# Quarter products in the free row tile of the score fills, and a narrower hold on VectorE's score tiles

## The chip, the cores and the metric

The kernel runs on one core of one Trainium2 chip. The metric is the device time of one execution in microseconds (us); the median of three runs before the change is 734.45 us (734.43 to 736.88). The core has five engines with instruction queues of their own: TensorE (PE in the profile) multiplies matrices into the accumulator memory PSUM, whose eight banks hold 128 x 512 float32 values each; ScalarE (ACT) applies functions such as exp; VectorE (DVE) does elementwise work and copies; GpSimd (POOL) does integer adds here; SyncE (SP) issues most of the DMAs. They meet at semaphores.

## The reference

Two layers are computed on separate inputs and joined along the last axis, each for 2048 positions and width 640. The first is a state-space layer: a complex diagonal recurrence over time between two dense products, plus a skip term. The second is attention with 32 query heads of width 20 that share one key and one value head.

```python
    Lam_bar = jnp.exp(dt * Lam)
    B_bar = ((Lam_bar - 1.0) / Lam)[:, None] * Bmat
    Bu = jnp.einsum("bld,pd->blp", x + 0j, B_bar)
    for t in range(L):
        h = Lam_bar[None, :] * h + Bu[:, t, :]
        hs.append(h)
    y = 2.0 * jnp.einsum("blp,dp->bld", hseq, Cmat).real + x * Dskip[None, None, :]
...
    q = (x @ wq) split into 32 heads of 20;  k = x @ wk;  v = x @ wv
    scores = jnp.einsum("bhqd,bkd->bhqk", q, k) * (Dh ** -0.5)
    p = _softmax(scores, axis=-1)
    o = jnp.einsum("bhqk,bkd->bhqd", p, v)
    b = (heads of o joined) @ wo
...
    return jnp.concatenate([a, b], axis=-1)
```

## The kernel before, in words

**Score tiles.** Attention is cut into 2048 score tiles of 128 keys x 512 queries: four blocks of 512 queries, eight groups of four heads, sixteen key chunks, four heads. A head needs only 20 (plus one) of the 128 input rows of TensorE, so the four heads of a group lie in four bands of 32 rows of the tiles KT and QT, and a score matmul uses one *row tile*: 32 rows by 128 columns of the array (32*128 in the profile). `fill` issues the score matmuls of two or three tiles, in different row tiles, into one of two PSUM slots (SC, three banks each).

**Two ways to exp.** Either ScalarE applies exp to a slot (L1213, PR<-SC: 1024 or 1536 columns for two or three tiles). Or VectorE turns the score into the bits of a power of two in int16 (`fill_d`, BIG<-SC); three further shifted copies follow, on GpSimd two tiles at a time (L1507) or on VectorE, and the weighted sum of the four approximates exp. The names with `_d` and the third tile of a slot called `own` stand for this. A tile done by ScalarE needs one value product, one done by VectorE needs four. Value products use *column tiles*, 128 rows by 32 columns (128*32), four heads side by side (`pv`, MB<-PR,VP and MB<-BIG,VS), and add up in one bank, `pvbank`.

**Everything else on TensorE** runs in column tiles too: `mm` splits a product with 128 output rows into four matmuls of 32. These are the products of generator tasks: `q_task` (queries, 5 steps of 128 input rows each), `unit_task` (input of the recurrence for one of four time blocks and one of five state chunks: 10 steps for each of real and imaginary part), `cb_task` (a product of C and B, 10 steps), `y_task` (output of the state-space layer, up to 16 steps, where the fifth of each block, k = 4, handles the last 128 columns), `o_task` (output projection, 5 steps), and some small ones. Each holds a PSUM bank (MB) until VectorE has copied it out. Two single banks are left beside the slots: `pvbank`, and one for all tasks (`misc`).

**The order of all instructions is written out before the run.** `Schedule` simulates the engines with estimated durations, picks by priority what each engine does next, and the `Emitter` writes every engine's stream and the semaphore waits. Score fills have priority 0, tasks 0.95, value products 2.0 (0.9 when they are urgent). An operation has a mode, S for row tiles and C for column tiles, and changing the mode has a price in the plan. Tasks come up by the number of score tiles issued (`tile_n`), the state-space work between tiles 260 and 1780; `planned` tries several random shifts of these times (`PLANS`, 4) and keeps the plan that ends first by its own clock.

**How many tiles VectorE gets.** `want_own` and `want_d` allow one when the count stays under `SHARE` (0.28) of the tiles, when buffers are free, when fewer than two first steps wait, and when `behind()` is false. `behind()` (L1273) is true while the closing step W of the next state-space unit hasn't started and `tile_n` is more than 120 tiles (`LAG`) past that unit's due time. VectorE steps of a unit have low priority until `hurry` marks them `late`, 40 tiles after the due time (scaling of C: from tile 150).

Of the kernel before, what the change touches and what calls it, by code (L numbers as in the profile page):

```python
# [23 lines left out]
class Op:  # L24
# [3 lines left out]
                 "seq", "land", "dma_key", "idx", "tail", "mode", "load", "late", "port", "after", "due", "table", "psum")  # L28

    def __init__(self, eng, fns, dur, deps=(), prio=5, reads=(), writes=(), prev=None, gate=None, hook=None,  # L30
# [7 lines left out]
        self.port, self.after, self.due, self.table = port, [], None, None  # L38
# [213 lines left out]
class Emitter:  # L252
# [11 lines left out]
    def plan(self):  # L264
# [8 lines left out]
        for op in self.order:  # L273
# [12 lines left out]
            for o in op.after:  # L286
                dep(o)
            for k in op.writes:
                for k2 in self.shares.pop(k, ()):
                    dep(last_w.get(k2))  # L290
                    for r in readers.get(k2, ()):
                        dep(r)
# [55 lines left out]
        for e in ("pe", "act", "dve", "pool"):  # L348
            v = 0
            for op in self.streams[e]:  # L350
                if op.dma_key is None and id(op) in needed:
                    v += 1
                    self.value[id(op)] = v
# [4 lines left out]
    def emit(self, block):  # L358
        def run(e, be):
            for op in self.streams[e]:  # L360
# [6 lines left out]
                for fn in op.fns:  # L367
                    ins = fn(be)
                    if op.dma_key is not None:
# [14 lines left out]
class Bank:  # L384
# [7 lines left out]
    def cols(self, lo, hi):  # L392
        return self.tensor[:, self.off + lo:self.off + hi]

# [21 lines left out]
class Build:  # L416
# [7 lines left out]
    SHARE = 0.28  # L424
# [66 lines left out]
    PLANS = 4  # L491
# [149 lines left out]

    @staticmethod
# [12 lines left out]
    def program(self):  # L655
# [7 lines left out]
        self.tasks = []  # L663
        self.evac_op, self.norm_op, self.part_op = {}, {}, {}
# [362 lines left out]
    def q_task(self, qb, blk, bank):  # L1027

        p = self
        prev = None  # L1030
        for c in range(NC):
            at = 640 * c + 128 * blk
            prev = self.pe([self.mm(bank.ap, p.wqf[:, at:at + 128], p.xbT[:, c, 512 * qb:512 * qb + 512], c == 0, c == NC - 1)],
                           self.mmt(512), deps=[self.wqa_op, self.wq_op, self.xb_op[qb, c]] + bank.last, prev=prev,
                           prio=self.task_prio(), reads=[f"xbT{qb}_{c}", "wqa", "wqb"], writes=[bank.key])
# [143 lines left out]
    def fill(self, op, i):  # L1179
# [27 lines left out]
        for m in extra:  # L1207
            self.fill_d(op, m)
        op.reads = sorted(set(op.reads))
        op.dur = self.mmt(512, len(op.fns))  # L1210
        op.load = 128.0 * len(op.fns)
# [61 lines left out]
    def behind(self):  # L1273

        while self.next_unit < NQB * NC:
            w = self.w_op.get(divmod(self.next_unit, NC))
            if w is None or w.start is None:
                return self.tile_n > self.unit_due[divmod(self.next_unit, NC)] + self.LAG
# [405 lines left out]
    def o_task(self, qb, k, bank, early=False):  # L1684
# [28 lines left out]
        for i in range(begin, upto):  # L1713
            if last:
                yield lambda: all(n in self.norm_op for n in steps[i][0])
            prev = part(i, prev, i == begin)
        if early:
# [273 lines left out]
    def cb_task(self, cd, h, pc, ld, made, bank):  # L1991
        p = self
        prev = None
        n = 0
        for c in range(NC):
            for ri in range(2):
                prev = self.pe([self.mm(bank.cols(0, 320), pc[:, c, ri, :], p.CT[:, ri, c, 320 * h:320 * h + 320], n == 0, n == 2 * NC - 1)],
                               self.mmt(320), deps=[ld] + self.c_scaled + bank.last, prev=prev, prio=self.task_prio(),
                               reads=[f"pc{cd % 2}", f"CT{ri}_{c}"], writes=[bank.key])
                n += 1  # L2000
# [8 lines left out]
    def unit_task(self, tb, c, bank):  # L2009
        p = self  # L2010
        u = (tb * NC + c) % 2
        prev = None
        lo = 256 * (tb % 2)
        for ri in range(2):
            terms = [(eo, cd) for eo in range(2) for cd in range(NC)]
            for n, (eo, cd) in enumerate(terms):
                t, k, op = (p.BT, "BT", self.bt_op) if eo else (p.BA, "BA", self.ba_op)
                prev = self.pe([self.mm(bank.cols(256 * ri, 256 * ri + 256), t[:, ri, cd, 128 * c:128 * c + 128], p.xaT[:, cd, eo, lo:lo + 256],
                                        n == 0, n == 2 * NC - 1)], self.mmt(256),
                               deps=self.xa_op[tb] + [op[ri][cd]] + bank.last, prev=prev,  # L2020
                               prio=self.task_prio(), reads=[f"{k}{ri}_{cd}", f"xaT{tb % 2}_{cd}_{eo}"], writes=[bank.key])
# [68 lines left out]
    def y_task(self, tb, k, bank):  # L2090
# [3 lines left out]
        prev = None  # L2094
        rows_of = range(4) if k == 4 else [k]
        lo, hi = (512, 640) if k == 4 else (0, 512)
        W = p.W[tb % 2]
        for r in rows_of:
            i, eo = divmod(r, 2)
            o0 = 128 * r if k == 4 else 0  # L2100
            to = bank.cols(o0, o0 + hi - lo)
            x0 = 256 * (tb % 2) + 128 * i
            at = 1 + 128 * i + eo
            n = 0
            for c in range(NC):
                for ri in range(2):
                    m, mk = (p.CT, f"CT{ri}_{c}") if eo else (p.CA, f"CA{c}")
                    prev = self.pe([self.mm(to, W[:, c, ri, at:at + 128], m[:, ri, c, lo:hi], n == 0, False)],
                                   self.mmt(hi - lo), deps=deps, prev=prev,
                                   prio=self.task_prio(), reads=[f"W{c}_{tb % 2}", mk], writes=[bank.key])  # L2110
                    n += 1
            if not eo:
                for cd in range(NC):
                    prev = self.pe([self.mm(to, p.xaT[:, cd, 0, x0:x0 + 128], self.cb_of(cd, lo, hi), False, False)],
                                   self.mmt(hi - lo), deps=deps, prev=prev, prio=self.task_prio(),
                                   reads=[f"xaT{tb % 2}_{cd}_0", f"CB{cd}"], writes=[bank.key])
# [182 lines left out]
```

## Time and profile before

| | |
|---|---|
| median of 3 runs | 734.45 us |
| profiled execution: time, and its span | 734.64 us, 732.8 us |
| busy: PE, ACT, DVE, POOL | 708.3, 712.4, 602.0, 408.8 us |
| exponentials on ScalarE, L1213 | 679 |
| score matmuls, 32*128 | 2048 |
| value products, 128*32: MB<-PR,VP and MB<-BIG,VS | 1526 and 2088 |
| first steps on VectorE, BIG<-SC, 128x512 int16 | 485 |
| granted TensorE clock | 0.993 |

The page gives busy time and the chain that ended last; groups are listed as line, engine, operation, output<-input by tile name (buffer numbers left out), shape and count, then busy time, mean duration of one, idle time before them and what ended it. A table by stretch gives the window and its length, the busy time and count, the granted clock, and two DMA figures. In order of time, a row is: start, length, engine, line, operation, tiles, the tile of the array (rows*columns), shape, how many in a row. Line numbers are often those of helpers: L637 is the plain matmul, L633 the one split into four column tiles, L647, L651 and L652 are VectorE's elementwise helpers. A matmul's shown length of about 0.39 us includes the pipeline; the distance between starts tells what it occupies.

### The profile page before, as it was taken

What the parts mean: (1) busy time and instruction counts of PE and PEld (TensorE: products, weight loads), DVE (VectorE), ACT (ScalarE), POOL (GpSimd) and SP (SyncE); (2) the same over time, 40 slices, a digit from 0 to 9 for tenths busy, and PEclk for the clock granted to TensorE, in tenths of its full rate; (3) what the DMA queues carried; (4) which work ended last, traced back from release to release, by engine and by line L of the source; (5) the groups of instructions that cost most, each with busy time, mean ns of one, the idle gap of its engine ahead of it and who ended that gap; (6) DMA issues with size and microseconds to landing.
All of it is one profiled execution on the core that took longest, in us unless ns stands there. A gap on an engine that the chain in (4) does not pass through costs nothing.

```text
span 732.8 us, 26675 instructions
## 1 busy us (share of the span) xinstructions
PE 708.3 (97%) x11268; PEld 253.0 (35%) x11271; DVE 602.0 (82%) x1178; ACT 712.4 (97%) x703; POOL 408.8 (56%) x686
## 2 busy tenths in 40 slices
PE   8999999998999999999999999999999999999997
PEld 4322223233443432333333333233333333342233
DVE  7767999897677697778988998988889998876873
ACT  6899999999999999999999999999999999999995
POOL 3366564530046377586663746566645665687860
PEclk9799999999999999999999999999999999999999
DMA  9403543366121010100110010101100001100001
GB/s 204 68 27 107 133 110 99 76 138 97 31 60 26 13 30 24 38 23 18 40 41 23 16 26 26 42 21 34 34 20 10 19 8 40 37 24 18 19 21 38
DMA packets 78090, 34.44 MB, mean 47 GB/s; under 512 B 58852, under 2 KB 77972, under 8 KB 77972
## 3 DMA queue, kind: packets, MB, share of 16 engines
q1 hardware_dynamic: 76352, 32.34, 18.6%
q8 instruction: 90, 1.47, 0.8%
q10 hardware_dynamic: 1620, 0.39, 0.3%
q14 instruction: 28, 0.23, 0.1%
HBM read 11.53 MB, written 9.75 MB: 29 GB/s over the span
## 4 chain that ended last, share of the span: by engine, by line
ACT 52%; PE 45%; DVE 2%; DMA 1%; issue 1%; ACTq 0%
ACT PR L1213 51%; PE MB L637 16%; PE SC L637 15%; PE MB L633 12%; PE SC L633 1%; DMA BIG<-in_B_wq_dram 1%; DVE prod L647 0%; DVE BIG L652 0%; DVE mab L887 0%; DVE pvsb L647 0%; PE SC L929 0%; ACTq L618 0%; DVE g L2041 0%; DVE QT L652 0%; DVE pvsb L1574 0%
## 5 line engine op out<-in xcount | busy, mean ns | idle before, releaser
L1213 ACT ACTIVATE PR<-SC 128x1024 bf16<-128x1024 f32 (+1 forms) x679 | 697.5, 1239 | 5.1 <-PE SC L637 3.6
L1507 POOL INT64_ADD BIG<-BIG x659 | 397.9, 619 | 292.5 <-DVE BIG L652 171.8
L652 DVE TENSOR_SCALAR BIG<-SC 128x512 int16<-128x512 f32 x485 | 325.8, 686 | 70.1 <-PE SC L637 64.3
L637 PE MATMUL SC<-QT,KT 32*128 32x512 bf16 x2011 | 267.1, 386 | 14.6 <-ACT PR L1213 10.1
L637 PE MATMUL MB<-BIG,VS 128*32 128x512 bf16 x2088 | 244.0, 384 | 0.0
L637 PE MATMUL MB<-PR,VP 128*32 128x512 bf16 x1526 | 211.6, 386 | 0.5 <-DVE pvsb L1574 0.3
L637 PEld LDWEIGHTS SC<-QT,KT 32*128 32x128 bf16 x2011 | 68.0, 91 | 254.4 <-ACT PR L1213 178.1
L637 PEld LDWEIGHTS MB<-BIG,VS 128*32 128x32 bf16 x2088 | 59.1, 95 | 64.8 <-issue 47.3
L637 PEld LDWEIGHTS MB<-PR,VP 128*32 128x32 bf16 x1526 | 51.6, 95 | 54.8 <-issue 41.5
L652 DVE TENSOR_SCALAR BIG<-BIG 128x1024 int16<-128x1024 int16 (+1 forms) x136 | 48.8, 405 | 7.6 <-PE MB L637 5.7
L633 PE MATMUL MB<-CT,W 128*32 128x320 bf16 (+2 forms) x1040 | 51.4, 301 | 0.8 <-DVE prod L647 0.5
L633 PE MATMUL MB<-xaT,BT 128*32 128x256 bf16 x800 | 35.4, 275 | 0.0
L647 DVE TENSOR_TENSOR prod<-MB,tab 128x1024 bf16<-128x1024 f32 x20 | 24.3, 1217 | 13.0 <-PE MB L633 12.9
L633 PE MATMUL MB<-xaT,BA 128*32 128x256 bf16 x800 | 32.7, 274 | 0.0
L633 PE MATMUL MB<-CA,W 128*32 128x512 bf16 (+1 forms) x640 | 32.0, 302 | 0.7 <-issue 0.4
L652 DVE TENSOR_SCALAR BIG<-MB 128x512 int16<-128x512 f32 x37 | 25.2, 682 | 3.7 <-PE MB L637 2.4
L633 PE MATMUL MB<-WO,OP 128*32 128x128 bf16 (+1 forms) x576 | 27.8, 297 | 0.2 <-DVE pvsb L647 0.2
L633 PEld LDWEIGHTS MB<-CT,W 128*32 128x32 bf16 x1040 | 20.9, 96 | 18.2 <-issue 10.2
L633 PE MATMUL MB<-BIG 128*32 128x512 bf16 x340 | 26.7, 397 | 0.0
L1755 DVE CAST stg<-MB 128x512 bf16<-128x512 f32 x35 | 23.9, 683 | 1.7 <-PE MB L633 1.3
L1574 DVE CAST pvsb<-MB 128x512 bf16<-128x512 f32 x31 | 21.2, 684 | 3.8 <-PE MB L637 3.7
L2041 DVE TENSOR_TENSOR_SCAN g<-sc,hst,prod 128x256 bf16<-128x256 f32 x30 | 22.3, 754 | 0.1
(162 smaller groups left out, 388.2 us busy)
## 6 DMA issues: line engine op xcount, KB each, us to landing
out_dram<-stg SPq DMA_DIRECT2D x31, 128.0 KB, 1.8
qd<-BIG SPq DMA_DIRECT2D x20, 128.0 KB, 1.9
QT<-qd SPq DMA_DIRECT2D x28, 80.0 KB
OP<-pvsb SPq DMA_DIRECT2D x105, 20.0 KB
rdP<-recs SPq DMA_DIRECT2D x105, 20.0 KB
W<-in_A_B_re_dram SPq DMA_DIRECT2D x10, 160.0 KB, 2.6
W<-in_A_B_im_dram SPq DMA_DIRECT2D x10, 160.0 KB, 2.6
lbd<-W SPq DMA_DIRECT2D x10, 160.0 KB, 2.4
```

Source lines behind the costliest of these rows:

```text
L633: r = e.matmul(out[32 * j:32 * j + 32], lhsT=lhsT[:, 32 * j:32 * j + 32], rhs=rhs, start=start, stop=stop, tile_position=(0, 32 * j), skip ...
L637: return lambda e: e.matmul(out, lhsT=lhsT, rhs=rhs, start=start, stop=stop, **kw)
L647: return lambda e: e.tensor_tensor(out, a, b, op)
L652: return lambda e: e.tensor_scalar(out, a, s1, s2, op0=op0, op1=op1)
L1213: ex = self.act(lambda e: e.activation(dst, t[:, 0:512 * n], ACT.Exp, scale=1.0 / UNIT), 0.8333 * 512 * n + 64, table="exp", deps=[op], re ...
L1507: op.fns.append(lambda e: e.int64_add(words(dst), words(src), add))
L1574: ev = self.dve(lambda e: e.tensor_copy(p.pvsb[:, slot, :], bank.ap), 645, deps=[op], reads=[bank.key], writes=[f"pvsb{slot}", f"pvsb{slot ...
L1755: ev = self.dve(lambda e: e.tensor_copy(st, bank.ap), 645, deps=[prev], reads=[bank.key], writes=[key], prio=self.EV, gate=(lambda: last.e ...
L2041: o = self.dve(lambda e, ri=ri, init=init: e.tensor_tensor_scan(p.g[:, u, ri, :], rdec, p.prod[:, 1, 0, ri, :], init, ALU.mult, ALU.add), ...
```

## The change

A task of `q_task`, `o_task` (all but the last query block), `cb_task`, `unit_task` and `y_task` hands its steps to a new generator `ride`. It issues them from the front in column tiles, as before, in pieces of up to 256 columns. In addition `fill` calls `board` once its own tiles are chosen: if a row tile is still free, a step from the *back* of the list may be opened and split into four quarters of 32 input rows. One quarter, in the free row tile, joins the fill: its first matmul ahead of the scores, the others after them. A step is opened only when the product has begun, more than `KEEP_C` = 5 steps are left and none is open (`OPEN` = 1). When the steps run out, the task waits for the fills to take the quarters that are left; after 2500 ns of plan time (`PATIENCE`) one goes alone (`alone`). Consecutive quarters of a product write the same bank from different row tiles, so each waits on TensorE's own semaphore for the former (`fence`). Where a quarter has several matmuls, the operation increments its semaphore twice, at the last score and at the last matmul (`twice`), and waits of others count both. `behind()` gets a second condition. `SHARE` becomes 0.29 and `PLANS` 8. In `unit_task` and the narrow `y_task` the order of the terms changes, since a step now holds both parts or all four row blocks.

```diff
+            if op.fence is not None:
+                need[e] = op.fence
...
-                    v += 1
+                    v += 1 if op.twice is None else 2
...
-                for fn in op.fns:
+                for x, fn in enumerate(op.fns):
                     ins = fn(be)
+                    if x == op.twice and id(op) in self.needed:
+                        ins.then_inc(self.sems[e], 1)
...
-    SHARE = 0.28
+    SHARE = 0.29
...
-    PLANS = 4
+    PLANS = 8
...
+    GRAIN, KEEP_C = 256, 5
+    def ride(self, bank, steps):
+        p = self
+        r = Ride(bank, [[list(m), list(deps), list(keys)] for m, deps, keys in steps])
+        self.rides.append(r)
+        def hook(op):
+            mms, _, keys = r.steps[0]
+            n = 0
+            while mms and (not n or n + mms[0][2].shape[-1] <= p.GRAIN):
+                out, lhsT, rhs = mms.pop(0)
+                n += rhs.shape[-1]
+                op.fns.append(p.product(r, out, lhsT, rhs, range(4), r.last is None))
+                r.last = op
...
+        while r.open:
+            t0 = self.s.t
+            self.s.at(t0 + self.PATIENCE)
+            op = self.pe([], self.mmt(512), prio=1.5, mode="S", load=128.0, writes=[bank.key], hook=lambda op: self.alone(r, op),
+                         gate=lambda: bool(r.open) and self.s.t >= t0 + self.PATIENCE - 1.0)
...
+    def piece(self, r, out, lhsT, rhs, row):
...
+        at = slice(32 * row, 32 * row + 32)
+        return lambda e: e.matmul(out, lhsT=lhsT[at], rhs=rhs[at], start=False, stop=r.end is tag,
+                                  tile_position=(32 * row, 0), skip_group_check=True)
+    def board(self, op, used):
...
+            if best is None and rows and len(r.steps) > self.KEEP_C and len(r.open) < self.OPEN:
+                step = r.steps[-1]
+                if all(d.end is not None and s.seen(d, "pe") <= s.t for d in step[1]):
+                    best = [r.steps.pop(), set(range(4))], rows[0]
+                    r.open.append(best[0])
...
+            fns = [self.piece(r, *m, x) for m in step[0]]
+            if len(fns) > 1:
+                op.twice = len(op.fns)
+            op.fns[:] = fns[:1] + op.fns + fns[1:]
...
+            self.rode(r, op, x)
...
+    def rode(self, r, op, row):
+        if r.rode is not None:
+            op.fence = r.rode
+        r.rode = r.last = op
...
+        n_mm = len(op.fns)
+        self.board(op, used)
         op.reads = sorted(set(op.reads))
-        op.dur = self.mmt(512, len(op.fns))
-        op.load = 128.0 * len(op.fns)
+        op.dur = self.mmt(512, n_mm + (len(op.fns) > n_mm))
+        op.load = 128.0 * n_mm
...
-                return self.tile_n > self.unit_due[divmod(self.next_unit, NC)] + self.LAG
+                return self.tile_n > self.unit_due[divmod(self.next_unit, NC)] + self.LAG \
+                    and any(o.late and self.s.ready(o) is not None for o in self.s.pending["dve"])
...
+        prev = yield from self.ride(bank, [
+            ([(bank.ap, p.wqf[:, 640 * c + 128 * blk:640 * c + 128 * blk + 128], p.xbT[:, c, 512 * qb:512 * qb + 512])],
+             [self.wqa_op, self.wq_op, self.xb_op[qb, c]], [f"xbT{qb}_{c}", "wqa", "wqb"]) for c in range(NC)])
...
+        prev = yield from self.ride(bank, [
+            ([(bank.cols(0, 320), pc[:, c, ri, :], p.CT[:, ri, c, 320 * h:320 * h + 320])],
+             [ld] + self.c_scaled, [f"pc{cd % 2}", f"CT{ri}_{c}"]) for c in range(NC) for ri in range(2)])
...
+                steps.append(([(bank.cols(256 * ri, 256 * ri + 256), t[:, ri, cd, 128 * c:128 * c + 128],
+                                p.xaT[:, cd, eo, lo:lo + 256]) for ri in range(2)],
...
+        prev = yield from self.ride(bank, steps)
```

## The prediction

> **What bounds the kernel now.** I read the page first: the busy line, the chain that ended last, and the costliest groups.
>
> ```profile
> PE 708.3 (97%) x11268; PEld 253.0 (35%) x11271; DVE 602.0 (82%) x1178; ACT 712.4 (97%) x703; POOL 408.8 (56%) x686
> ...
> ACT 52%; PE 45%; DVE 2%; DMA 1%; issue 1%; ACTq 0%
> ```
>
> Two engines are full, and the chain passes from one to the other. ScalarE has hardly a hole: the exponentials (L1213) show 5.1 us idle in 697.5 busy. How they are split decides the time, so next the groups kept apart by shape:
>
> ```profile
> L1213 ACT ACTIVATE PR<-SC 128x1024 bf16<-128x1024 f32 x509 | 480.5, 1119 | 4.9 <-PE SC L637 3.6 <-PE MB L637 0.3
> ...
> L652 DVE TENSOR_SCALAR BIG<-SC 128x512 int16<-128x512 f32 x485 | 325.8, 686 | 70.1 <-PE SC L637 64.3 <-PE MB L637 0.9 <-POOL BIG L1507 0.2
> ...
> L1213 ACT ACTIVATE PR<-SC 128x1536 bf16<-128x1536 f32 x169 | 236.9, 1606 | 0.2 <-PE MB L637 0.2
> ```
>
> A fill brings three score tiles. Either ScalarE takes all three (1536 columns), or two, and VectorE the third (1024). ScalarE took 1526 of the 2048 tiles (2 x 509 + 3 x 169 + 1), so VectorE took 522. Then the stages. GpSimd's adds (L1507), which follow every VectorE tile, by stretch, and the exponentials from 153.8 to 202 and from 460 to 700:
>
> ```profile
> 20.00:153.00 133.00, 72.58 (x120) 0.96 0.36 90
> 153.00:203.00 50.00, 0.12 (x1) 1.00 0.43 88
> 203.00:480.00 277.00, 168.81 (x280) 1.00 0.12 29
> 480.00:720.00 240.00, 156.42 (x259) 1.00 0.09 23
> ...
> L1213 ACT ACTIVATE PR<-SC 128x1536 bf16<-128x1536 f32 x37 | 49.8, 1712 | 0.0
> ...
> L1213 ACT ACTIVATE PR<-SC 128x1024 bf16<-128x1024 f32 x201 | 188.4, 1115 | 1.0 <-PE SC L637 0.6
> L1213 ACT ACTIVATE PR<-SC 128x1536 bf16<-128x1536 f32 x41 | 58.3, 1554 | 0.2 <-PE MB L637 0.2
> ```
>
> For 50 us VectorE gets no score tile at all: `behind()` (L1273) holds them back. There a fill takes 49.8/37 = 1.346 us. From 460 to 700, where 201 of 242 fills (83%) have a VectorE tile, a fill of 1024 takes (240 - 41 x 1.346)/201 = 0.92. **So each tile moved to VectorE takes 0.42 us from ScalarE.** Last, TensorE in order of time:
>
> ```profile
> 360.30 0.39 PE L637 MATMUL SC<-QT,KT 32*128 32x512 bf16 x3
> 360.62 0.39 PE L637 MATMUL MB<-PR,VP 128*32 128x512 bf16 x1
> ...
> 361.17 0.39 PE L637 MATMUL SC<-QT,KT 32*128 32x512 bf16 x3
> 361.18 0.38 PE L637 MATMUL MB<-QT,KT 32*128 32x512 bf16 x1
> 361.49 0.39 PE L637 MATMUL MB<-PR,VP 128*32 128x512 bf16 x2
> ...
> 404.41 0.39 PE L637 MATMUL SC<-QT,KT 32*128 32x512 bf16 x3
> 404.64 0.38 PE L637 MATMUL MB<-QT,KT 32*128 32x512 bf16 x1
> 404.94 0.39 PE L637 MATMUL MB<-PR,VP 128*32 128x512 bf16 x2
> ...
> 654.49 0.83 PE L637 MATMUL MB<-BIG,VS 128*32 128x512 bf16 x12
> 655.25 0.39 PE L637 MATMUL SC<-QT,KT 32*128 32x512 bf16 x3
> ```
>
> Three score matmuls of 32 rows start together; 0.32 us later the column-tiled work starts (360.62). A group of four column matmuls takes (0.83 - 0.39)/2 = 0.22 (0.217 over longer runs), and from the last group's start to the next fill is 0.32, that is 0.10 for the change of tiling. A fourth row tile (361.17) leaves the distance at 0.32 (361.49): the free row costs under 0.01 us. From 203 to 720 TensorE shows 511 us busy of 517, so there it binds as well; from 153 to 203 it ran 164 dummy matmuls to stay warm.
>
> **The change, part by part.** *Hold.* From the starts of the 20 closing steps of the state-space units (W<-prod) and the number of score matmuls begun by then, `behind()` was true for 111 us in all. The new condition also wants a late VectorE step whose forerunners have started. From 153.8 to 178.0 VectorE works through exactly such a chain (scaling of C), and between a unit's rotation (prod<-MB) and its W another one stands ready. What is left open is where VectorE waits for TensorE: 178.0 to 181.4, 186.2 to 189.7, 194.2 to 197.6, 241 to 248.4, 386.4 to 389.5 and 527 to 532, about 25 us. That is 25/1.346 = 18.6 fills, of which 83% get a VectorE tile: 15 x 0.42 = **-6.5**. Ends: 0 if something late is always ready; all 111 us (82 fills, 68 tiles), but the new share 0.29 x 2032 = 589 allows 67: -28. I take the value of the gaps, since the timeline shows them.
>
> *Rides.* A quarter of a step leaves the column-tiled stage and goes in a fill's free row. 628 of 679 fills have just three row tiles. A step can be opened only after the product's first step and while more than five are left (KEEP_C = 5), one at a time (OPEN = 1). Query and output products have five steps, so by the code **they never ride**. For the others I took each product's matmuls, counted the fills between its steps, and opened a step by that rule: 20 units give 80 rides, the 10 CB products 28, the 16 wide y products 104, the four narrow ones 24: 236. A ride saves a quarter of 0.217, so 0.054 (CB, 320 columns: (0.85 - 0.30)/4/4 = 0.034): 208 x 0.054 + 28 x 0.034 = 12.2 us, less 236 x 0.004 for the fourth row, 11.2 us of TensorE; 28 of them lie before 203, where it isn't full: 10 us count. ScalarE is full too, so it must be exchanged: a 1024 fill with its VectorE tile costs TensorE 0.32 + 0.10 + 1.5 groups = 0.745, a 1536 fill 0.32 + 0.10 + 0.75 groups = 0.583, so one exchange needs 0.163 more TensorE in a round that is 0.42 shorter: 0.58. 10/0.58 = 17 exchanges x 0.42 = **-7**. What hides the new VectorE work: 32 tiles x 0.686 = 22 us more on an engine with 131 us idle, and 48 adds x 0.62 = 30 on GpSimd with 292 idle. Without that cover nothing is won here.
>
> A ride of a unit is two matmuls of 256 in one row tile, of the diagonal and the narrow products up to four of 128, and the exponential waits for the last one (two increments). Below: full-array matmuls of 128 columns, new weights each, ran 16 in 1.07 us, (1.07 - 0.22)/15 = 0.057, so four take 0.23, as long as a score. Above: the one kind of fill here with a late fourth matmul (404.41, fourth at 404.64, next group 404.94) took 0.53 instead of 0.32, so 0.21 a ride. I take the lower, a row with the same column counts, and keep 0.21 for the range.
>
> A rule of the Trainium skill speaks against this part ("TensorEngine Tiling (Array Packing)", Instruction Overhead): every matmul carries an overhead of some 60 cycles, so no tiling factor should come out of a dimension that is already small. At the 2.4 GHz of the table in "TensorE: Matmul & The Clock Gate" that is 25 ns; for some 580 pieces of 128 to 512 columns I estimate 14.5 us, so that the rides would cost TensorE 3 us instead of saving 11, and the sum would end near 731. The measured 0.057 for 128 columns is only 4 ns above 128 cycles at that clock, so I go by the row.
>
> *Waits.* Each ride waits on TensorE for the ride before (fence); behind it stand the fill, and for that ScalarE. The former fill's matmuls end 0.39 after their start and fills are 0.87 or more apart, so 0; above, 0.1 each if the release is late, 24. Quarters left when the steps run out wait 2.5 us (2.7 fills) for a matching free row, then run alone for 0.22; the row left out is the one with most tiles left and comes first next time, so I take 5, **+1**; a quarter of all would be +13. Meanwhile the one spare bank is held, and the next product with its evacuation and output DMA on SP waits; the code adds or moves no other DMA.
>
> *Share 0.28 to 0.29* binds only from about 60 to 110 us (D share 0.25 to 0.27 of the tiles): 0.01 x 300 = 3 tiles, **-1**. *Eight plans for four*: the planner takes the best by its own clock; 0 to -2, I take 0. Finer steps (256 columns at a time) issue the same matmuls: 0.
>
> **Sum**: the profiled execution took 734.64 (span 732.8, 1.8 around it), 0.2 over the median 734.45. 734.6 - 6.5 - 7 - 1 + 1 = **721**.
>
> **Rivals.** (1) *VectorE takes everything*: with the hold gone and TensorE relieved, the share is reached: 67 x 0.42 = 28, so 706 to 711. For it: outside the hold 83% of fills already have a VectorE tile. Against: VectorE would get to (602 + 46)/706, 92%, and TensorE needs 67 x 0.58 = 39 us for it.
> (2) *Pieces in one row tile do not overlap* (slower): the fill grows by up to 0.21, 236 rides, and the next exponential is late. From 0.10 a ride on it loses: 236 x (0.10 - 0.05) = 12, more than the hold's 7.5 and the 0.5%; 0.11 gives 741, 0.21 765. For it: the fill at 404.41. Against: the 0.057 row.
> (3) *The units slip* (slower): the hold also kept most units at 100 to 150 tiles behind their due times, and no more. The last y product now ends at 708.6, the last exponential at 722.6: 14 us of room. A slip of over 80 us, a full block of five y products after the last score (5 x 16 x 0.217 + 3 = 20), gives 741.
> (4) *Nothing is exchanged*: the freed TensorE time becomes dummy work and something late is always ready, so the hold stays: 730 to 734.
>
> **How the numbers follow.** The forecast 0.55 (its own range 714 to 728), rival 1 0.15, rival 2 0.10, rival 3 0.07, rival 4 0.13. About 0.5% (3.7 us) is what a measurement can tell from no change. Faster by more: 0.55 + 0.15 + 0.05 of rival 4 = 0.75; within: 0.08; slower: 0.17. The range must reach from rival 1 to the near end of rivals 2 and 3: 706 to 740, which leaves out most of rival 2 and some of rival 3, some 0.13.
>
> **What would show it.** Exponentials of 1024 columns rise from 509 to some 545, those of 1536 fall to about 145; GpSimd's adds no longer vanish from 178 to 203 but still do from 154 to 178. Some 240 quarters appear as 32*128 matmuls of W, xaT, CA, CT in fills, none of wq or WO, and fills with them still take 0.32 to the next group. Wrong if such fills take 0.4 or more, if y products stand after the last exponential, or if the 1024 count stays below 515.

## The result, and the profile after

The changed kernel takes **728.31 us** (median of 4, 727.54 to 729.73) against 734.55 before (median of 4): a ratio of **0.990, 95% interval 0.987 to 0.993**, 6.2 us less by the medians, 7.2 by the ratio. The forecast was 721: the direction is right, the gain about half of what was forecast (13.5).

**The clock of an execution.** The executions of one kernel don't all run at the same granted TensorE clock, and their times follow it. The 25 executions of the kernel before that were measured with four of the experiments took 738.1 to 738.8 us at 0.986, 735.7 to 736.8 at 0.990, 733.9 to 736.05 at 0.993 and 733.0 to 734.1 at 0.995. The changed kernel took 727.5 and 727.6 at 0.992 and 0.993, so at the same clock too the gain is some 7 us. The two profiled executions differ in this as well (0.993 before, 0.987 after). Each page shows where, in tenths of full speed by slices of 18 us:

```profile
PEclk9799999999999999999999999999999999999999
PEclk9789999999999999999999999999999999999999
```

In the traces the clock is halved for 10.2 us before (27.4 to 37.7) and for 17.1 us after (9.4 to 12.8 and 26.5 to 40.1); from 45 us to the end of the score tiles it is full in both. So two profiles are best compared from 45 us on.

First the page after: the busy line and the chain by engine.

```profile
PE 698.2 (96%) x11257; PEld 250.8 (34%) x11260; DVE 608.9 (84%) x1188; ACT 706.9 (97%) x703; POOL 417.0 (57%) x702
...
ACT 64%; PE 33%; DVE 2%; issue 0%; POOL 0%
```

TensorE is busy 10.1 us less, but the span is only 4.9 us shorter (727.9): the time in which TensorE does nothing rose from 24.5 to 29.7 us. ScalarE is as full as before, and the chain now runs on it for 64% of the span instead of 52%. So part of what TensorE was given went idle. The groups by shape say how the tiles are split:

```profile
L1347 ACT ACTIVATE PR<-SC 128x1024 bf16<-128x1024 f32 x522 | 491.3, 1126 | 4.5 <-PE SC L649 4.2 <-PE MB L649 0.2
...
L786 DVE TENSOR_SCALAR BIG<-SC 128x512 int16<-128x512 f32 x498 | 335.5, 687 | 78.6 <-PE SC L649 72.4 <-PE MB L649 1.1
...
L1347 ACT ACTIVATE PR<-SC 128x1536 bf16<-128x1536 f32 x157 | 219.8, 1584 | 0.1
```

ScalarE took 2 x 522 + 3 x 157 = 1515 of 2048 tiles, VectorE 533: 11 more than before (522), where the forecast had some 32. Next GpSimd's adds by stretch (window, length, busy time and count, granted clock, two DMA figures):

```profile
20.00:153.00 133.00, 65.66 (x109) 0.95 0.36 87
153.00:203.00 50.00, 7.70 (x13) 1.00 0.41 89
203.00:480.00 277.00, 175.91 (x292) 1.00 0.12 30
480.00:720.00 240.00, 156.91 (x262) 1.00 0.09 23
```

and the exponentials from 153.8 to 202 (first two lines) and from 460 to 700:

```profile
L1347 ACT ACTIVATE PR<-SC 128x1536 bf16<-128x1536 f32 x31 | 42.3, 1613 | 0.0
L1347 ACT ACTIVATE PR<-SC 128x1024 bf16<-128x1024 f32 x9 | 9.0, 1226 | 0.0
...
L1347 ACT ACTIVATE PR<-SC 128x1024 bf16<-128x1024 f32 x208 | 194.4, 1110 | 0.2 <-PE MB L649 0.2
L1347 ACT ACTIVATE PR<-SC 128x1536 bf16<-128x1536 f32 x37 | 52.5, 1538 | 0.1
```

In the stretch that was empty, VectorE now gets nine tiles. All of them start at 182.9 or later, when the scaling of C is done.

**Where the time went.** From the first exponential to the end of the span, before took 732.8 - 20.4 = 712.4 us and after 727.9 - 21.95 = 705.95, 6.4 less. It splits like this. The shortest usual distance from one exponential to the next is 0.903 us after 1024 columns and 1.330 after 1536, so 13 more of the one and 12 fewer of the other make -4.2. The time above these distances, which I call ScalarE's waits, fell from 16.9 to 15.75: -1.2. In the first 45 us they rose from 3.6 to 4.7, with the longer stretch of halved clock; from 45 us on they fell from 13.3 to 11.0. All waits of ScalarE below are those from 45 us on. The end behind the last exponential fell from 10.7 to 9.7: -1.0. In the profiled execution the first exponential starts 1.5 us later than in that of before, which is why the spans differ by only 4.9.

**How a ride looks.** The groups of the quarters, then TensorE in order of time around a fill that carries a quarter of a unit, and around one that carries a quarter of the diagonal step of a y product:

```profile
L729 PE MATMUL MB<-diagD,xaT 32*128 32x128 bf16 x320 | 31.4, 217 | 0.0
L729 PE MATMUL MB<-xaT,BT 32*128 32x256 bf16 x160 | 30.9, 272 | 0.3
...
L729 PE MATMUL MB<-CT,W 32*128 32x320 bf16 x32 | 9.7, 304 | 0.7 <-ACT PR L1347 0.6
L729 PE MATMUL MB<-BIG,xaT 32*128 32x512 bf16 x12 | 4.6, 384 | 0.0
...
L729 PE MATMUL MB<-BIG,xaT 32*128 32x128 bf16 x16 | 2.2, 219 | 0.0
```

```profile
407.80 0.28 PE L729 MATMUL MB<-xaT,BT 32*128 32x256 bf16 x1
407.80 0.39 PE L649 MATMUL SC<-QT,KT 32*128 32x512 bf16 x3
407.92 0.27 PE L729 MATMUL MB<-xaT,BT 32*128 32x256 bf16 x1
408.12 0.73 PE L719 MATMUL MB<-xaT,BA 128*32 128x256 bf16 x20
...
665.70 0.22 PE L729 MATMUL MB<-diagD,xaT 32*128 32x128 bf16 x1
665.70 0.39 PE L649 MATMUL SC<-QT,KT 32*128 32x512 bf16 x3
665.76 0.33 PE L729 MATMUL MB<-diagD,xaT 32*128 32x128 bf16 x3
666.02 0.61 PE L719 MATMUL MB<-CT,W 128*32 128x512 bf16 x8
```

The count is 212 quarters: 320/4 = 80 diagonal steps, 160/2 = 80 of units, 32 of CB products, 12 and 16/2 = 8 of second steps of y. None is of wq or WO. The first piece starts with the three scores, the next one 0.12 or 0.06 us later in the same row tile, and the column-tiled work starts 0.32 us after the scores, as without a ride. Over all such fills the distance is 325 ns with a quarter, of two pieces or four, and 321 ns without.

### The profile page after: what moved, and what is told of

The parts are those of the page before. It is cut to its first block, busy times and chain, and to the rows that moved or that the text cites. A ratio compares the mean times of both kernels' runs of the same rounds, so it can differ in the third digit from the quotient of the medians.

```text
span 727.9 us, 26720 instructions
## 1 busy us (share of the span) xinstructions
PE 698.2 (96%) x11257; PEld 250.8 (34%) x11260; DVE 608.9 (84%) x1188; ACT 706.9 (97%) x703; POOL 417.0 (57%) x702
## 3 DMA queue, kind: packets, MB, share of 16 engines
HBM read 11.53 MB, written 9.75 MB: 29 GB/s over the span
## 4 chain that ended last, share of the span: by engine, by line
ACT 64%; PE 33%; DVE 2%; issue 0%; POOL 0%
ACT PR L1347 63%; PE MB L649 12%; PE SC L649 9%; PE MB L719 8%; PE MB L729 3%; DVE BIG L786 1%; PE MB L645 1%; PE SC L645 0%; PE SC L1064 0%; PE SC L719 0%; DVE mab L1022 0%; ACT L1964 0%; DVE stg L1896 0%; DVE pvsb L1709 0%; ACT BIG L1007 0%
## 5 line engine op out<-in xcount | busy, mean ns | idle before, releaser
L1642 POOL INT64_ADD BIG<-BIG x675 | 406.2, 616 | 278.8 <-DVE BIG L786 153.4
L786 DVE TENSOR_SCALAR BIG<-SC 128x512 int16<-128x512 f32 x498 | 335.5, 687 | 78.6 <-PE SC L649 72.4
L649 PE MATMUL MB<-BIG,VS 128*32 128x512 bf16 x2132 | 254.0, 384 | 0.1
L649 PE MATMUL MB<-PR,VP 128*32 128x512 bf16 x1515 | 216.7, 387 | 0.2 <-ACT PR L1347 0.2
L719 PE MATMUL MB<-CA,W 128*32 128x512 bf16 (+1 forms) x640 | 36.2, 302 | 0.1
L729 PE MATMUL MB<-diagD,xaT 32*128 32x128 bf16 x320 | 31.4, 217 | 0.0
L729 PE MATMUL MB<-xaT,BT 32*128 32x256 bf16 x160 | 30.9, 272 | 0.3
L729 PEld LDWEIGHTS MB<-diagD,xaT 32*128 32x128 bf16 x320 | 17.7, 92 | 28.4 <-ACT PR L1347 21.5
L719 PE MATMUL MB<-xaT,BT 128*32 128x256 bf16 x640 | 26.6, 274 | 0.0
```

Source lines behind the costliest of these rows:

```text
L649: return lambda e: e.matmul(out, lhsT=lhsT, rhs=rhs, start=start, stop=stop, **kw)
L719: x = e.matmul(out[32 * j:32 * j + 32], lhsT=lhsT[:, 32 * j:32 * j + 32], rhs=rhs, start=start, stop=r.end is tag, tile_position=(0, 32 * ...
L729: return lambda e: e.matmul(out, lhsT=lhsT[at], rhs=rhs[at], start=False, stop=r.end is tag, tile_position=(32 * row, 0), skip_group_check ...
L786: return lambda e: e.tensor_scalar(out, a, s1, s2, op0=op0, op1=op1)
L1642: op.fns.append(lambda e: e.int64_add(words(dst), words(src), add))
```

## The experiments

The expectations call the theories by letters and say there what each would give. **A** is the reading of the two traces: both parts bring much less than forecast by themselves, since the units slip when the hold is narrowed, and since time freed on TensorE is worth less than was taken. Its rival is the prediction's own working, with its sizes. Two forms of A came up for the rides. **A1**: a product that waits for its quarters holds the one spare bank for longer. **A3**: the rides of the first time block fall where TensorE isn't the limit and only delay the units there, so that the hold lasts longer. Where tiles are counted, it is the score tiles that VectorE takes.

### The rides with the old hold

```diff
-                return self.tile_n > self.unit_due[divmod(self.next_unit, NC)] + self.LAG \
-                    and any(o.late and self.s.ready(o) is not None for o in self.s.pending["dve"])
+                return self.tile_n > self.unit_due[divmod(self.next_unit, NC)] + self.LAG
```

> The changed kernel with the old condition of behind(), so rides without the narrower hold. Theory A (the hold decides how many score tiles VectorE gets, and rides alone hardly change it): exponentials of 1024 columns 509 to 517, some 210 quarters, 733 us (732 to 735). Theory B (the gain is TensorE's time that the rides free, 11 us by 0.72): 728 to 730, nearly the whole gain, and over 520 exponentials of 1024. Theory C (the gain is the hold's alone): 734 to 735.

Measured: 734.25 us against 735.71, ratio 0.998 (0.9963 to 0.9997), 1.5 us less. VectorE takes 528 tiles. 204 quarters ride, and free 9.75 us of TensorE by the prediction's own prices; almost nothing comes of it.

### The hold alone

```diff
 # before.py
-                return self.tile_n > self.unit_due[divmod(self.next_unit, NC)] + self.LAG
+                return self.tile_n > self.unit_due[divmod(self.next_unit, NC)] + self.LAG \
+                    and any(o.late and self.s.ready(o) is not None for o in self.s.pending["dve"])
```

> The kernel before with only the second condition in behind(); no rides, share 0.28, four plans. Theory A: the hold opens in gaps but the units fall further behind and it is true for longer, so 515 exponentials of 1024 and 732 us (731 to 733.5). Theory B: 734 to 735. Theory C: 728 to 729, 520 or more exponentials of 1024.

Measured: 733.43 against 735.71, ratio 0.9972 (0.9957 to 0.9987), 2.1 us less, 528 tiles; ScalarE's waits are 13.4 us (13.3 before). Six more tiles at 0.42 are 2.5 us, so the price of a tile holds and the number of tiles doesn't: the forecast had 15 tiles and 6.5 us for this part.

### Everything but the rides

```diff
-    OPEN = 1
+    OPEN = 0
```

> The changed kernel with OPEN = 0: everything but the rides. Theory A: between, 730 to 732, so that rides and hold together bring more than the two alone. Theory B: 733 to 735. Theory C: 728 to 729, as the changed kernel.

Measured: 733.59 against 735.71, ratio 0.9963 (0.9946 to 0.998), 527 tiles, waits 12.5. Eight of its twelve executions ran at a clock of 0.986 to 0.988. The four at 0.993 have a median of 731.4; at that clock the hold alone has 732.6 and the kernel before 734.7. So A's 730 to 732 is met at equal clock, and the new share, the eight plans and the finer steps together bring about 1 us, which the ratios alone don't resolve.

These three tell where the tiles went. VectorE's score tiles by the stretch in which they start, and below them the time in which the *old* condition was true (worked out, as in the prediction, from the starts of the W steps and the score matmuls begun by then):

| us | before | hold alone | all but rides | rides, old hold | after |
|---|---|---|---|---|---|
| 20 to 153 | 96 | 94 | 99 | 99 | 99 |
| 153 to 203 | 0 | 11 | 7 | 0 | 9 |
| 203 to 400 | 145 | 144 | 150 | 137 | 152 |
| 400 to 480 | 74 | 68 | 60 | 74 | 62 |
| 480 to the end | 207 | 211 | 211 | 218 | 211 |
| sum | 522 | 528 | 527 | 528 | 533 |
| old condition, 203 to 400 | 47 | 89 | 131 | 59 | 179 |
| old condition in all | 111 | 168 | 231 | 125 | 270 |

The narrowed hold does open the gaps after 183. But the tiles it lets in push the units back. These are the rotations of the first units (DVE in order of time: start, length, line, operation, tiles, and in brackets VectorE's idle time before), before, with the hold alone, and after:

```profile
181.44 1.23 DVE L647 TENSOR_TENSOR prod<-MB,tab 128x1024 bf16<-128x1024 f32 x1 [3.37 <-PE MB L633]
189.71 1.23 DVE L647 TENSOR_TENSOR prod<-MB,tab 128x1024 bf16<-128x1024 f32 x1 [2.37 <-PE MB L633]
197.56 1.23 DVE L647 TENSOR_TENSOR prod<-MB,tab 128x1024 bf16<-128x1024 f32 x1 [3.13 <-PE MB L633]
```

```profile
185.91 1.21 DVE L647 TENSOR_TENSOR prod<-MB,tab 128x1024 bf16<-128x1024 f32 x1
195.38 1.22 DVE L647 TENSOR_TENSOR prod<-MB,tab 128x1024 bf16<-128x1024 f32 x1
202.84 1.22 DVE L647 TENSOR_TENSOR prod<-MB,tab 128x1024 bf16<-128x1024 f32 x1
```

```profile
185.90 1.21 DVE L781 TENSOR_TENSOR prod<-MB,tab 128x1024 bf16<-128x1024 f32 x1
197.03 1.21 DVE L781 TENSOR_TENSOR prod<-MB,tab 128x1024 bf16<-128x1024 f32 x1
209.83 1.21 DVE L781 TENSOR_TENSOR prod<-MB,tab 128x1024 bf16<-128x1024 f32 x1
```

VectorE's idle 2.4 to 3.4 us are gone, as forecast, but the units slip. The first three follow each other at 8.3 and 7.9 us before, at 9.5 and 7.5 with the hold alone, and at 11.1 and 12.8 after, where their own quarters delay them as well (see the last two experiments). Times from the start of the span also move with the clock, so count score tiles: the sixth unit's W starts 150 tiles after its due time before, 170 with the hold alone, 201 with all but the rides and 264 after. The condition that the hold starts from is true for 111 us before, 168 with the hold alone and 270 after. The rule then refuses tiles later on: from 400 to 480 VectorE takes 6 fewer with the hold alone and 12 fewer after. In the written order the rule refuses a tile at 89 fills before and at 93 after. The hold was moved rather than shortened.

### No hold at all

```diff
-                return self.tile_n > self.unit_due[divmod(self.next_unit, NC)] + self.LAG \
-                    and any(o.late and self.s.ready(o) is not None for o in self.s.pending["dve"])
+                return False
```

> The changed kernel with behind() always false. Theory A: VectorE gets all that the share allows, about 580 tiles, the units slip, y products stand after the last exponential and the time grows to 750 to 765, though ScalarE has 20 us less to do. Theories B and C (what limits is TensorE's time or the hold itself): 45 tiles more by 0.42, 705 to 715.

Measured in one round: 762.35 us (two executions), ratio 1.037 (1.033 to 1.040). VectorE takes 582 tiles, and ScalarE is done early; the page's busy line, and ScalarE at the end in order of time:

```profile
PE 716.2 (94%) x11391; PEld 258.9 (34%) x11391; DVE 657.9 (87%) x1315; ACT 688.0 (91%) x695; POOL 420.1 (55%) x700
```

```profile
713.44 0.38 ACT L1713 ACTIVATE pvsb<-MB 128x256 bf16<-128x256 f32 x1 [0.56 <-PE MB L649]
755.84 0.60 ACT L1890 ACTIVATE PR<-SC 128x512 bf16<-128x512 f32 x1 [42.01 <-PE SC L645]
```

TensorE meanwhile, from 712.7 on:

```profile
712.67 0.28 PE L719 MATMUL SC<-xaT,BA 128*32 128x256 bf16 x4
712.78 0.39 PE L719 MATMUL SC<-CA,W 128*32 128x512 bf16 x4
```

Units and y products are left over when the scores are done, and stand alone for 42 us. This is the mechanism of the prediction's third rival, and it shows what the hold buys: 49 more tiles than after (49 x 0.42 = 21 us off ScalarE), paid with more than that at the end. In the change itself it doesn't occur: the last y product ends at 701.2, before the last exponential.

### Less work for TensorE alone

From the kernel before, the C times B product's term is left out of the y products (the products themselves are still made). That takes 40 column groups of 512 columns and 40 of 128 from TensorE: 40 x 0.217 + 40 x 0.053 = 10.8 us.

```diff
 # before.py, y_task
-            if not eo:
+            if False:
                 for cd in range(NC):
```

> The kernel before, with the product of C and B times x left out of y (five steps of every second y product: 4 x (2 x 5 + 2 x 5 / 4) = 50 groups of 0.217, 10.8 us of TensorE; the output lacks this term). It frees as much TensorE time as the rides do, without their waiting. Theory A1 (freed TensorE time is worth something under the old hold too, and the rides lose it again because a product that waits for its last quarters holds the only spare bank): 4 us less than before, some 533 tiles on VectorE. Theory A2 (TensorE doesn't limit under the old hold): 1 to 2 us less, as with the rides under the old hold. Theory B (TensorE limits, 0.72 of it counts): 8 us less.

Measured: 730.5 against 734.99, ratio 0.9932 (0.9906 to 0.9958): by the ratio 5.0 us less (3.1 to 6.9), 0.46 for each us freed (0.29 to 0.64). VectorE takes 533 tiles. The busy line and the exponentials of 1024 columns, in this kernel:

```profile
PE 702.0 (96%) x11004; PEld 247.4 (34%) x11004; DVE 612.7 (84%) x1205; ACT 708.9 (97%) x701; POOL 410.3 (56%) x688
...
L1213 ACT ACTIVATE PR<-SC 128x1024 bf16<-128x1024 f32 x514 | 485.0, 1111 | 6.5 <-PE SC L637 4.7 <-PE MB L637 1.0
```

The 11 more tiles are exchanged at 0.42, as forecast, and ScalarE's waits hardly change (14.0 us for 13.3). What falls short is the number: at the prediction's 0.58 us of TensorE for each exchange, 10.8 us would pay for 18, and 11 were made. The rest went idle: TensorE does nothing for 29.6 us (731.6 - 702.0), 5.1 more than before, as in the changed kernel (29.7). Why no more exchanges were made isn't shown here.

### Less work for VectorE alone

From the kernel before, the cross terms are left out of the scaling of C: 10 steps for 40, about 15 us of VectorE.

```diff
 # before.py, the scaling of C
-            a = self.scaled(xa, x, sc[:, self.G2RE, c:c + 1], sc[:, self.G2IM, c:c + 1], True, ...)
-            b = self.scaled(x, x, sc[:, self.GRE, c:c + 1], sc[:, self.GIM, c:c + 1], True, ...)
+            a = [self.dve(self.ts(xa, x, sc[:, self.G2RE, c:c + 1], None, ALU.mult), 470, ...)]
+            b = [self.dve(self.ts(x, x, sc[:, self.GRE, c:c + 1], None, ALU.mult), 470, ...)]
```

> The kernel before, with the cross terms left out of the scaling of C (10 VectorE steps for 40, some 15 us off the chain that runs from 152 to 178; CA and CT are scaled by the real part alone). If VectorE's own late chain sets the length of the hold (theory A): the 40 us without a score tile shrink by some 12, 8 to 10 tiles more on VectorE, 3 to 4 us less than before. If the hold is set by the units' TensorE steps and the bank: 0 to 1 us less.

Measured: 734.09 against 734.99, ratio 0.9976 (0.9958 to 0.9994), 1.8 us less. The chain by engine, and the exponentials of 1024 columns:

```profile
PE 58%; ACT 38%; DVE 2%; DMA 1%; issue 1%; ACTq 0%
...
L1213 ACT ACTIVATE PR<-SC 128x1024 bf16<-128x1024 f32 x523 | 494.4, 1100 | 8.0 <-PE SC L637 6.0 <-PE MB L637 1.0
```

VectorE takes 534 tiles, 12 more and one more than in the changed kernel, and yet almost nothing is won: ScalarE's waits rise to 16.6 us (13.3 before). Tiles without relief of TensorE turn into waits for TensorE, and the chain now lies on TensorE for 58%. A VectorE tile brings four value products where ScalarE's brings one; that these make TensorE late is my reading. A count of tiles is no measure of the time. The changed kernel is faster at 533 tiles because its waits are 11.0.

### More rides

```diff
-    GRAIN, KEEP_C = 256, 5
+    GRAIN, KEEP_C = 256, 1
```

> The changed kernel with KEEP_C = 1, so that query and output products ride too: some 340 quarters for 212. Theory A1 (a ride frees TensorE but holds the bank until its last quarter finds a row): slower than the changed kernel by 6 to 10, 734 to 739, and the units further behind. Theory B (TensorE's freed time counts): 128 x 0.05 x 0.72 = 5 us less than the changed kernel.

Measured: 736.77 against 734.99, ratio 1.0017 (0.9999 to 1.0035), some 8.5 us slower than the changed kernel although a third more quarter matmuls ride (720 for 540) and VectorE takes 536 tiles. ScalarE waits for scores more than twice as long:

```profile
L1347 ACT ACTIVATE PR<-SC 128x1024 bf16<-128x1024 f32 x520 | 490.3, 1111 | 10.7 <-PE SC L649 10.0
```

Its waits are 20.5 us, for 11.0 in the changed kernel. Of the difference, 5.1 us are one hole before the exponential at 73.61, in which TensorE makes query products one after another and the next scores wait. Only here do query products ride; whether that made them late isn't shown. After their last column step the units wait 18.4 us in sum for their last quarters and the y products 12.2; in the changed kernel 3.8 and 3.9. So the price that A1 names exists, and `KEEP_C` = 5 keeps it small; what part of the 8.5 us it makes isn't separated.

### A later hold

```diff
-    LAG = 120
+    LAG = 160
```

> The changed kernel with LAG = 160 for 120: the hold begins 40 tiles later. Theory A (the hold trades VectorE tiles against the slip of the units, with a flat best near here): 4 to 6 tiles more on VectorE, 726 to 728.5, last y product no later than the last exponential. Without such a trade: 40 tiles later on 10 units would be 15 tiles, 6 us less.

Measured: 728.74 against 734.99, ratio 0.9899 (0.9869 to 0.9929), 539 tiles, waits 13.6: the same time as the changed kernel. Six more tiles (2.5 us) and 2.6 us more waits cancel.

### Rides only where TensorE is full, with both holds

The quarters of the first time block's units and of the CB products stay in column tiles; the rest ride as in the change. First with the old hold:

```diff
-    def ride(self, bank, steps):
+    def ride(self, bank, steps, may=True):
...
-        self.rides.append(r)
+        if may:
+            self.rides.append(r)
...
-                return self.tile_n > self.unit_due[divmod(self.next_unit, NC)] + self.LAG \
-                    and any(o.late and self.s.ready(o) is not None for o in self.s.pending["dve"])
+                return self.tile_n > self.unit_due[divmod(self.next_unit, NC)] + self.LAG
...
-        prev = yield from self.ride(bank, steps)
+        prev = yield from self.ride(bank, steps, tb > 0)
```

> As the rides under the old hold, but the five units of the first time block and the CB products, which come up while fills are 1.35 us apart and TensorE has time to spare, take no rides: some 164 quarters for 212. Theory A3 (rides alone gained so little because there a product waits for four fills 1.35 apart, 4.9 to 5.5 us instead of 3.3, so the first units and with them the hold end later): 4 to 5.5 us less than before, near 730, some 535 tiles on VectorE and the first rotations at 181 to 205 as before. If a quarter of the rides less only means less TensorE time freed: 734, as with all rides under the old hold or a little more.

Measured: 730.05 against 736.54, ratio 0.9928 (0.9904 to 0.9951): 5.3 us less by the ratio, with 164 quarters. With *more* rides (204) and the same hold it was 1.5. The next fences show why. TensorE in order of time, with all rides and the old hold, at the end of the first unit:

```profile
180.65 0.28 PE L729 MATMUL MB<-xaT,BT 32*128 32x256 bf16 x1
...
181.99 0.28 PE L729 MATMUL MB<-xaT,BT 32*128 32x256 bf16 x1
...
182.98 0.28 PE L719 MATMUL MB<-xaT,BT 128*32 128x256 bf16 x4
183.34 0.28 PE L729 MATMUL MB<-xaT,BT 32*128 32x256 bf16 x1
```

A quarter goes with each fill, and in this stretch fills are 1.35 us apart: the column steps are done at 182.98, and the last quarter has to wait for the next fill. The rotations of the first three units in this kernel, and then in the one without the early rides:

```profile
183.81 1.22 DVE L781 TENSOR_TENSOR prod<-MB,tab 128x1024 bf16<-128x1024 f32 x1 [2.81 <-PE SC L649]
193.22 1.23 DVE L781 TENSOR_TENSOR prod<-MB,tab 128x1024 bf16<-128x1024 f32 x1 [4.15 <-PE SC L649]
202.62 1.23 DVE L781 TENSOR_TENSOR prod<-MB,tab 128x1024 bf16<-128x1024 f32 x1 [4.39 <-PE SC L649]
```

```profile
184.10 1.23 DVE L783 TENSOR_TENSOR prod<-MB,tab 128x1024 bf16<-128x1024 f32 x1 [3.15 <-PE MB L721]
191.78 1.23 DVE L783 TENSOR_TENSOR prod<-MB,tab 128x1024 bf16<-128x1024 f32 x1 [2.27 <-PE MB L721]
199.62 1.22 DVE L783 TENSOR_TENSOR prod<-MB,tab 128x1024 bf16<-128x1024 f32 x1 [2.52 <-PE MB L721]
```

With early rides the units are 9.4 us apart, VectorE idle for up to 4.4 of them, and what releases it is a fill (PE SC); without, they are 7.7 and 7.8 apart, and it is a column step (PE MB). The time from a unit's first matmul to its rotation is 4.9, 5.3 and 5.5 us with early rides and was 3.3 before. The old hold lasts 125 us with them and 108 without, and VectorE takes 528 and 536 tiles. This is A3. A1, as the reason for the small gain under the old hold, falls: the sum of the times from first matmul to copy is 116 us for the units there and was 120 before, and for the y products 161 and 190. A rival is that one written order is luckier than another. The plan's own clock speaks against it: with the old hold, the eight plans with all rides end at 722.6 to 724.9 us, the eight without the early ones at 717.7 to 722.0.

The same restriction with the new hold:

```diff
-        prev = yield from self.ride(bank, steps)
+        prev = yield from self.ride(bank, steps, tb > 0)
```

(and the same `may` and CB products as above.)

> The changed kernel (narrower hold) with the same restriction of the rides. Theory A3: the narrower hold already lets VectorE work while the first units wait for quarters, so little is left to win: 0 to 1 us less than the changed kernel, 727 to 728.5. If the first rides' wait cost the changed kernel as much as the old hold: 3 to 4 less, 724 to 725.

Measured: 728.15 against 736.54, ratio 0.9905 (0.988 to 0.9931), 535 tiles: the same as the changed kernel. Where VectorE may use the gap, the longer wait for quarters costs nothing that can be measured. So, once the early rides are taken out, the parts add up as far as can be told: 5.3 for the rides and, between the two kernels of this pair, 1.9 for the hold, which alone gave 2.1. The intervals of the pair overlap, and the plan's own clock differs by up to 3 us between the eight plans of one kernel (715.8 to 718.8 for the changed one), so a difference of 1 or 2 us between two kernels can also be one of plans. No version was measured to beat the changed kernel.

## Why the prediction was half right

- **The price of a ride: right.** 0.004 us was taken, 325 - 321 = 4 ns measured, whatever the pieces. Rival 2 (pieces in one row tile don't overlap, up to 0.21) is refuted, and with it the sum near 731 that followed from the Trainium skill, "TensorEngine Tiling (Array Packing)", Instruction Overhead: the 540 pieces in the fills cost less than 1 us in all (212 x 0.004), where the estimate by that rule, read as a cost added for every matmul, had 14.5.
- **Which steps ride: right.** None of queries and output, as the code's `KEEP_C` said; 212 quarters for 236.
- **Hold, -6.5: mis-sized, it gave about -2** (0.9972 alone, 1.9 us between the two kernels of the last pair). The step that failed is "what is left open is where VectorE waits for TensorE ... about 25 us". The gaps were read in the trace of before as though the units would stay where they were. The condition is a control loop: the tiles let into a gap delay the units, the units' lag keeps the rule at work, and it refuses later what it allowed earlier (89 fills against 93). So 6 tiles were won and not 15; at 0.42 they make the 2 us or so that were measured, and ScalarE's waits stayed the same. Rival 3 had named the slip, but only as a catastrophe at the end.
- **Rides, -7: mis-sized.** On top of the rest of the change they gave 0.9963 to 0.9902, about 4.5 us; with the old hold 1.5 as made, 5.3 without the early ones. The freed time was about right (212 quarters free 9.75 us by the same prices). Two steps failed. "10/0.58 = 17 exchanges x 0.42", 0.72 us of time for each us freed, took it that all freed time is exchanged: the direct measurement gives 0.46 (0.29 to 0.64), since 11 exchanges were made for 18 and 5 us of TensorE went idle. Here too 11 tiles were exchanged, with both parts together, and about a third of the gain is shorter waits and a shorter end, for which the sum had no term. Nor had it one for the waits that more tiles bring where TensorE isn't relieved: 3.3 us for 12 tiles with less work for VectorE, 2.6 for 6 with the later hold. And "28 of them lie before 203, where it isn't full" priced the early rides at nothing. They cost: under the old hold 3.8 us, the difference between 1.5 and 5.3, because a quarter waits for a fill and the unit with it. In the change as made the new hold hides that.
- **Waits of quarters, +1: small, as said, but not measured in time.** One quarter goes alone in the written order; the products wait 7.7 us in sum for their last quarters, most of it beside other work.
- **Share, -1, and plans, 0.** VectorE's tiles from 20 to 129 rise from 77 to 84 in the kernels with the new share and the finer steps (all but the one with `KEEP_C` = 1, which has 77), more than the 3 taken, but 4 are lost from 129 to 153. The time between the hold alone and all but the rides is about 1 us at equal clock, as forecast, with the finer steps in it. The plan kept is the first of the eight, so four would have given the same.
- **The signs given beforehand.** The 1024 count is above 515, where the prediction would have been wrong, but far from 545. The adds vanish from 154 to 178 and not from 183 to 203, as said; fills with quarters take 0.32; no y product stands behind the last exponential. They confirmed the mechanisms; the one that measured size, the 1024 count, already showed the miss.
- **The other rivals.** 1, VectorE takes everything: no, 533 tiles, not 589. 4, nothing exchanged: its reasons (freed time goes idle, something late is always ready) hold for about half of the expected gain: TensorE's idle time rose by 5.2 us of the 10.1 that it was relieved of.

## What to carry to other kernels

Where two or three engines are full at once, don't count time freed on one as if all of it were exchanged: here it was worth about half of itself. Leave work out of the kernel before to measure it directly, as was done here. Idle gaps under a rule that compares progress with due times are no stock of free time: what is let into them moves the progress, and the rule takes it back. Work that has to wait for a carrier belongs where the carrier comes often and its engine is the limit; elsewhere it only makes a chain longer. And before a wait in one profile is compared with that in another, compare the granted clock stretch by stretch: here some 2 us of ScalarE's waits went with the clock of the execution and not with the kernel.

## What the runs showed of the hardware that was not expected

Up to four matmuls of 128 columns one after another in a fourth row tile, beside three of 512 in the other row tiles, cost 4 ns (325 for 321 ns to the next column group), the same as two of 256 or one of 320 or 512.

The first exponential starts at 20.4 to 20.7 us in four of the profiles and at 21.4 to 22.3 in the others, a spread of nearly 2 us in the part of the program that the change hardly touches. The five latest (21.95 to 22.3) are the five whose granted clock is 0.66 to 0.74 between 10 and 15 us; in the other seven it is 1.00 there. What separates 20.4 to 20.7 from 21.4 to 21.8 stays open. It is why the two profiled spans differ by 1.5 us less than the work behind the first exponential.

The clock is halved while TensorE has work: from 30 to 40 us it is busy for 10.0 of 10 us in both profiles, at a granted clock of 0.62 before and 0.50 after. In the twelve profiles a halved stretch begins at 25 to 27.5 us, and the waits of ScalarE in the first 45 us go by its length, whatever the kernel: 3.3 to 3.6 us where it lasts 10.2 us (three profiles), 4.7 to 4.9 at 13.7 (five), 5.9 to 6.0 at 17.1 (four). What decides the length isn't shown; runs of one and the same kernel differ in their mean clock from 0.986 to 0.995, and by 5 to 6 us with it.
